# Sparse attention into a gated feed-forward layer: queries ordered by GpSimd, value maxima folded by VectorE, one lasting tile for value halves, first weight decoded in its own order

## The chip, the cores and the metric

One NeuronCore of a Trainium2 chip runs the whole program: TensorE (PE) multiplies, VectorE (DVE), ScalarE (ACT) and GpSimd (POOL) work elementwise, SyncE (SP) issues transfers. The metric is the device time of one execution in microseconds, the lower the better.

## The reference

Block-sparse attention over 4 batches, 8 heads, 768 positions and 64 channels, in 24 blocks of 32; then a feed-forward layer with a gate.

```python
scores = scale * np.matmul(q, k.transpose(0, 1, 3, 2))          # scale = 1/8
mask = (np.abs(blk_i - blk_j) <= 1) | (blk_i == 0) | (blk_j == 0) | (blk_i == 23) | (blk_j == 23)
for qb in range(24):                                            # and three drawn blocks a row
    for kb in sampled_blocks[qb]:
        mask[qb * 32:(qb + 1) * 32, kb * 32:(kb + 1) * 32] = True
attn = softmax(where(mask, scores, -1e9))
x = (attn @ v).transpose(0, 2, 1, 3).reshape(3072, 512)
h = x @ w_in                                                    # 512 x 2048
sp = np.maximum(h, 0.0) + np.log1p(np.exp(-np.abs(h)))
out = (h * erf(sp)) @ w_out                                     # 2048 x 512
```

The weights are float64, all else float32.

## The kernel before, in words

**Numbers.** Products of float32 accuracy are made from float16 halves: a value is scaled by a power of two and cut into a high half (a cast by ScalarE) and a low half (what is left, by VectorE), and three products of halves are added up in PSUM. Scores are float32 products.

**Weights.** Float64 weights arrive as pairs of 32-bit words, and `decode` (a `TENSOR_SCALAR` and two `SCALAR_TENSOR_TENSOR` on VectorE for each 1024 columns) puts float32 numbers together from them: 8 decodes for w_in (`key` is "i", i = 0, 2, ..., 14), 8 for w_out. Raw w_in lies partly in the places of w_out, so a w_out block is loaded (`load_w`, from ScalarE's queue) when the raw words there are decoded. `square` sums squares for the scales, `high` casts the high half (ScalarE), and the low half is made for w_in on TensorE: `rest` multiplies the float32 weight by a diagonal of scales, `rest_low` takes the high half off, `rest_out` casts. `weights()` is a generator; `later(n)` lets it go on by n steps.

**Attention.** A batch has 11 units of two query blocks each ("m") and 4 units for the first and last block ("f"); together 60 units. For a unit: `order_q` copies its queries from `qt`, the loaded tile, to `qm` (two tiles, used in turns; two copies of 64x256), `gather` copies the drawn key blocks `kg` (six copies on GpSimd for the unit's two blocks), `gather_v` loads value rows `vbuf` (SP, and an indirect transfer on GpSimd), `scores` writes `s_m` or `s_f` in PSUM, `soft_max` finds the row maximum `mx`, `soft_exp` the exponentials `pf` and their high half, `soft_low` the low half `p_m` and their transpose by DMA, `values` (three units later) writes `po`, `norm` divides (`rinv`, `xf`), `turn` cuts into halves and transposes.

**Values.** Values of the next batch are prepared while a batch runs (`behind`): `max_v` finds the largest magnitude of a batch's values, over the columns on VectorE and then over the 128 partitions, `scale_v` makes a power of two of it, `split_v` writes halves into a tile `vn`, with two columns of ones (a memset on GpSimd), and stores them to a table `vtab` in DRAM from which `gather_v` reads.

**Feed-forward.** x comes in 12 chunks of 256 rows; w_in's 2048 columns are taken in 8 groups of 256. `ff_first` writes h (24 products), `ff_logs`, `ff_power`, `ff_exp` and `ff_gate` compute the gate in turns on ScalarE and VectorE (tiles x, s, g), `ff_second` adds into o three groups later. That makes 96 groups in the main loop, and a table says in which iterations a unit of attention runs beside a group.

**Order.** Ahead of the loop six units and the weights run in an order that a scheduler sets for TensorE, ScalarE and VectorE; from the fourth iteration of the loop on these too follow the program. The queues of SP and GpSimd always do. A DMA queue waits at a transfer whose place is not free, and what stands behind it waits too. Every operation is recorded under one line, L47, so the rows below are told apart by tiles.

## Time and profile before

| | us |
|---|---|
| median of three executions (lowest, highest) | 804.48 (802.73, 805.50) |
| the profiled execution | 807.05 |
| its span in the trace | 804.5 |
| TensorE busy | 717.3 (89%) |
| VectorE busy | 646.8 (80%) |
| ScalarE busy | 601.0 (75%) |
| GpSimd busy | 209.2 (26%) |

The span reaches from the first to the last instruction that the trace holds, the execution's time has a little more around it. Busy shares are means over the whole span; the loop starts with the first h at 116 us, and the first o at 135 us.

### The profile page before, as it was taken

What the parts mean: (1) busy time and instruction counts of PE and PEld (TensorE: products, weight loads), DVE (VectorE), ACT (ScalarE), POOL (GpSimd) and SP (SyncE); (2) the same over time, 40 slices, a digit from 0 to 9 for tenths busy, and PEclk for the clock granted to TensorE, in tenths of its full rate; (3) what the DMA queues carried; (4) which work ended last, traced back from release to release, by engine and by line L of the source; (5) the groups of instructions that cost most, each with busy time, mean ns of one, the idle gap of its engine ahead of it and who ended that gap; (6) DMA issues with size and microseconds to landing.
All of it is one profiled execution on the core that took longest, in us unless ns stands there. A gap on an engine that the chain in (4) does not pass through costs nothing.

```text
span 804.5 us, 26510 instructions
## 1 busy us (share of the span) xinstructions
PE 717.3 (89%) x11136; PEld 505.3 (63%) x11136; DVE 646.8 (80%) x1215; ACT 601.0 (75%) x1035; POOL 209.2 (26%) x397
## 2 busy tenths in 40 slices
PE   1237888889977999999999899999999999999997
PEld 1235546656755777666767667667777776666663
DVE  5897999988878788887778888787888888775664
ACT  2556899678766788787857987887888788787674
POOL 2247721213334241500143424110344310000000
PEclk9658999989999999999999999999999999999999
DMA  9999853996699698953597998744598747312000
GB/s 307 405 196 321 245 110 74 210 214 156 135 234 213 146 243 183 198 122 81 131 195 169 201 240 182 167 110 102 126 188 179 155 115 172 74 33 43 8 27 26
DMA packets 187287, 129.46 MB, mean 161 GB/s; under 512 B 137760, under 2 KB 160928, under 8 KB 185376
## 3 DMA queue, kind: packets, MB, share of 16 engines
q1 hardware_dynamic: 173440, 83.98, 50.2%
q10 hardware_dynamic: 7840, 25.96, 10.2%
q0 software_dynamic: 5888, 17.84, 8.7%
q8 instruction: 87, 1.43, 0.7%
q14 instruction: 32, 0.26, 0.1%
HBM read 82.81 MB, written 12.95 MB: 119 GB/s over the span
## 4 chain that ended last, share of the span: by engine, by line
PE 68%; issue 11%; DVE 7%; DMA 4%; POOL 4%; ACT 3%; POOLq 1%; SPq 1%; ACTq 0%; DVEq 0%
PE h L47 27%; PE o L47 27%; PE s_m L47 7%; PE po_None L47 4%; PE s_f L47 3%; POOL vbuf L47 2%; POOL kg L47 2%; DMA qt<-in_qT_dram 2%; PE po L47 1%; DVE s L47 1%; DVE vn L47 1%; DVE p_m L47 1%; ACT x L47 1%; DMA vtab<-vn 1%; DMA pT_f<-p_f 1%
## 5 line engine op out<-in xcount | busy, mean ns | idle before, releaser
L47 PE MATMUL h<-xT,wi 128*128 128x256 f16 x2304 | 270.2, 274 | 7.1 <-DVE s L47 7.0
L47 PE MATMUL o<-wo,g 128*128 128x512 f16 x1152 | 268.4, 383 | 0.3 <-DVE g L47 0.2
L47 PEld LDWEIGHTS <-wi 128*128 128x128 f16 x2304 | 226.6, 99 | 56.3 <-issue 6.9
L47 PEld LDWEIGHTS <-g 128*128 128x128 f16 x1152 | 110.3, 99 | 123.8 <-issue 5.6
L47 POOL DMA_INDIRECT vbuf<-vtab,idx x88 | 94.7, 1076 | 322.4 <-PE po_None L47 254.5
L47 ACT ACTIVATE s<-s 128x512 f32<-128x512 f32 x192 | 120.1, 626 | 42.8 <-DVE s L47 33.5
L47 PE MATMUL s_m<-kx,qm 128*64 128x64 f32 (+1 forms) x1408 | 97.0, 250 | 35.9 <-DVE qm L47 17.2
L47 ACT ACTIVATE x<-x 128x512 f32<-128x512 f32 x192 | 121.1, 631 | 5.9
L47 POOL COPY kg<-kx 128x128 f32 x264 | 96.3, 412 | 69.9 <-PE s_m L47 54.5
L47 PEld LDWEIGHTS s_m<-kx,qm 128*64 128x64 f32 x1408 | 72.4, 148 | 42.6 <-issue 24.2
L47 ACT ACTIVATE pf_m<-s_m,nb_m 128x256 f32<-128x256 f32 x176 | 69.0, 475 | 38.7 <-DVE nb_m L47 38.5
L47 DVE SCALAR_TENSOR_TENSOR s<-x 128x512 f32<-128x512 f32 x96 | 67.5, 703 | 26.2 <-ACT x L47 26.1
L47 ACT ACTIVATE x<-h,isg 128x512 f32<-128x512 f32 x96 | 65.2, 679 | 30.7 <-PE h L47 30.6
L47 DVE SCALAR_TENSOR_TENSOR s<-s,s 128x512 f32<-128x512 f32 x96 | 67.7, 705 | 21.9 <-ACT s L47 18.5
L47 DVE SCALAR_TENSOR_TENSOR g<-s,sums,g 128x512 f16<-128x512 f32 x96 | 72.1, 751 | 3.4
L47 DVE TENSOR_REDUCE mx_m<-s_m 128x4 f32<-128x1024 f32 x44 | 53.7, 1221 | 23.2 <-PE s_m L47 22.9
L47 PE MATMUL s_m<-kg,qm 128*64 128x96 f32 x704 | 65.7, 261 | 6.7 <-issue 6.7
L47 DVE SCALAR_TENSOR_TENSOR s<-s,h 128x512 f32<-128x512 f32 x96 | 65.4, 681 | 0.5
L47 ACT ACTIVATE s<-x 128x512 f32<-128x512 f32 x96 | 60.4, 630 | 3.0
L47 DVE TENSOR_SCALAR g<-s,sums 128x512 f16<-128x512 f32 x96 | 47.4, 493 | 3.4
L47 DVE TENSOR_TENSOR p_m<-pf_m,p_m 128x1024 f16<-128x1024 f32 x38 | 49.5, 1303 | 0.4 <-ACT p_m L47 0.4
L47 PEld LDWEIGHTS s_m<-kg,qm 128*64 128x64 f32 x704 | 45.4, 149 | 5.5 <-issue 5.5
(109 smaller groups left out, 667.5 us busy)
## 6 DMA issues: line engine op xcount, KB each, us to landing
vbuf<-vtab SPq DMA_DIRECT2D x80, 195.0 KB, 4.5
vraw<-in_v_dram ACTq DMA_DIRECT2D x9, 768.0 KB
vtab<-vn SPq DMA_DIRECT2D x16, 390.0 KB, 3.3
vbuf<-vtab SPq DMA_DIRECT2D x12, 520.0 KB, 5.5
wo<-in_w_out_dram ACTq DMA_DIRECT2D x6, 1024.0 KB, 7.2
qt<-in_qT_dram SPq DMA_DIRECT2D x20, 256.0 KB
kr<-in_kT_dram ACTq DMA_DIRECT2D x12, 384.0 KB, 6.1
vbuf<-vtab SPq DMA_DIRECT2D x32, 130.0 KB, 6.2
```

The source lines that it names most:

```text
L47: done = call(*args, **kwargs)
```

## The change

Four parts. `order_q` runs on GpSimd for all units after the seventh of the first batch, and `next_queries` is cut in two: `order_next` (the copies) and `next_queries` (the loads), both called at the head of an iteration, ahead of its gathers, not at its end. For batches 1 to 3 the maximum over partitions is found by VectorE (`fold_bound`: transposes of 32x32 squares, reductions and copies) in place of a reduction by GpSimd. Where the halves of values went to a tile `vn` taken anew each time, there is one lasting tile, whose ones are set once. And w_in is decoded with its columns in the order in which they arrive, not with even and odd ones apart: `halves` reads the float32 numbers with a step instead, and `ff_first` counts columns accordingly.

```diff
--- before.py
+++ after.py
@@ -155,7 +155,9 @@
         qt = qts[b, t][:, :, half * 2 * BLOCK : (half + 1) * 2 * BLOCK].rearrange("p r (j c) -> p r j c", c=BLOCK)
         for a in range(2):
             place = qms[half][a * D : (a + 1) * D, :, :, a, :]
-            if b == 0 and 0 < u <= FIRST:
+            if b or u > FIRST:
+                pool.tensor_copy(place, qt[a * D : (a + 1) * D])
+            elif u:
                 act.activation(place, qt[a * D : (a + 1) * D], AF.Copy)
             else:
                 dve.tensor_copy(place, qt[a * D : (a + 1) * D])
@@ -181,23 +183,35 @@
 
     sums = cp.tile([P, 64], F32, tag="sums", name="sums")
 
-    def pow2_bound(bound, tag, by_sum):
+    def pow2_bound(bound, tag):
 
 
 
         top = st.tile([P, 1], F32, tag="top", name=f"top_{tag}")
         dve.reduce_max(top, bound, AX.X)
-        if by_sum:
-            allm = ps_h.tile([P, W], F32, tag="h", name=f"allm_{tag}")
-            if tag[0] == "v":
-                pe.matmul(allm[0:1, 1 : 1 + P], top, eye, start=True, stop=True)
-                top = st.tile([P, 1], F32, tag="top", name=f"most_{tag}")[0:1]
-                dve.reduce_max(top, allm[0:1, 1 : 1 + P], AX.X)
-            allm = allm[:, :1]
-            pe.matmul(allm, ones[: top.shape[0]], top, start=True, stop=True)
-        else:
-            allm = st.tile([P, 1], F32, tag="allm", name=f"allm_{tag}")
-            pool.partition_all_reduce(allm, top, P, bass.bass_isa.ReduceOp.max)
+        allm = ps_h.tile([P, W], F32, tag="h", name=f"allm_{tag}")
+        if tag[0] == "v":
+            pe.matmul(allm[0:1, 1 : 1 + P], top, eye, start=True, stop=True)
+            top = st.tile([P, 1], F32, tag="top", name=f"most_{tag}")[0:1]
+            dve.reduce_max(top, allm[0:1, 1 : 1 + P], AX.X)
+        allm = allm[:, :1]
+        pe.matmul(allm, ones[: top.shape[0]], top, start=True, stop=True)
+        return allm
+
+    def fold_bound(bound, tag):
+
+        one, other = fold[:, :BLOCK], fold[:, BLOCK:]
+        dve.reduce_max(one[:, :1], bound, AX.X)
+        dve.transpose(other, one)
+        most = st.tile([P, 5], F32, tag="most", name=f"most_{tag}", bufs=1)
+        for n in range(4):
+            dve.reduce_max(most[0:1, n : n + 1], other[n * BLOCK : n * BLOCK + 1], AX.X)
+        dve.reduce_max(most[0:1, 4:5], most[0:1, :4], AX.X)
+        dve.tensor_copy(other[0:1], most[0:1, 4:5].to_broadcast([1, BLOCK]))
+        dve.transpose(one[:BLOCK], other[:BLOCK])
+        allm = st.tile([P, 1], F32, tag="allm", name=f"allm_{tag}", bufs=1)
+        for n in range(4):
+            dve.tensor_copy(allm[n * BLOCK : (n + 1) * BLOCK], one[:BLOCK, :1])
         return allm
 
     def pow2_scale(allm, tag, squared):
@@ -224,6 +238,10 @@
         for quad in range(2):
             pool.dma_start(vtab[b][NB * BLOCK :, quad * QW : (quad + 1) * QW], zero16)
 
+    vn_of = cp.tile([P, KT, 2, VW], F16, tag="vn", name="vn_of")
+    pool.memset(vn_of[:, :, :, D : D + 2], 1.0)
+    fold = cp.tile([P, 2 * BLOCK], F32, tag="fold", name="fold")
+    dve.memset(fold, 0.0)
     vmax = {}
 
     def max_v(b, quad):
@@ -234,7 +252,7 @@
                 vmax[b][:, 4 * quad + h : 4 * quad + h + 1], vr, AX.X, apply_absolute_value=True
             )
         if quad == 1:
-            vscale[b] = pow2_bound(vmax[b], f"v{b}", b == 0)
+            vscale[b] = (fold_bound if b else pow2_bound)(vmax[b], f"v{b}")
 
     def scale_v(b):
         vscale[b] = pow2_scale(vscale[b], f"v{b}", False)
@@ -243,8 +261,11 @@
 
         s = vscale[b][0]
         place, bufs = ("vn", 1) if b else (("xT", 3), ("xT", 3), ("vn", 1), ("pf", 2))[2 * quad + half]
-        vn = (mo if place == "xT" else at).tile([P, KT, 2, VW], F16, tag=place, name=f"vn_{b}_{quad}_{half}", bufs=bufs)
-        pool.memset(vn[:, :, :, D : D + 2], 1.0)
+        if place == "vn":
+            vn = vn_of
+        else:
+            vn = (mo if place == "xT" else at).tile([P, KT, 2, VW], F16, tag=place, name=f"vn_{b}_{quad}_{half}", bufs=bufs)
+            pool.memset(vn[:, :, :, D : D + 2], 1.0)
         for a in range(2):
             vr = vraws[b, quad][half * 2 + a].rearrange("p (k d) -> p k d", d=D)
             hi, lo = vn[:, :, a, :D], vn[:, :, a, D + 2 :]
@@ -425,15 +446,7 @@
             dve.tensor_scalar(m, hi, 3, 0x3FFFFFFF, ALU.logical_shift_left, ALU.bitwise_and)
             dve.scalar_tensor_tensor(m, hi, -0x40000000, m, ALU.bitwise_and, ALU.bitwise_or)
             done = w32[:, c : c + w].bitcast(I32)
-            if key == "i":
-                lo, m = (x.rearrange("p (q e) -> p e q", e=2) for x in (lo, m))
-                done = done.rearrange("p (e q) -> p e q", e=2)
-            if key == "i" and i == 0:
-                part = mags[1][:, c : c + w]
-                dve.tensor_scalar(part.rearrange("p (e q) -> p e q", e=2), lo, 29, None, ALU.logical_shift_right)
-                dve.tensor_tensor(done, part.rearrange("p (e q) -> p e q", e=2), m, ALU.bitwise_or)
-            else:
-                dve.scalar_tensor_tensor(done, lo, 29, m, ALU.logical_shift_right, ALU.bitwise_or)
+            dve.scalar_tensor_tensor(done, lo, 29, m, ALU.logical_shift_right, ALU.bitwise_or)
             c += w
 
     def square(key, i):
@@ -444,7 +457,11 @@
 
     def halves(key, i):
         t, t16 = (wi, wi16) if key == "i" else (wo, wo16)
-        return t[:, i + APART[key], :], t16[:, i, :512], t16[:, i, 512:]
+        w32, hi16, lo16 = t[:, i + APART[key], :], t16[:, i, :512], t16[:, i, 512:]
+        if key == "i":
+            w32 = w32.rearrange("p (n q e) -> p n e q", n=2, e=2)
+            hi16, lo16 = (x.rearrange("p (n e q) -> p n e q", n=2, e=2) for x in (hi16, lo16))
+        return w32, hi16, lo16
 
     def scale_of(key, i):
         n = i // (2 * NK) if key == "i" else i // 2
@@ -481,7 +498,7 @@
         scale_part(total, n)
 
     def bound_part(part):
-        return pow2_bound(wsq["i"][:, part * NK : (part + 1) * NK], f"wi{part}", True)
+        return pow2_bound(wsq["i"][:, part * NK : (part + 1) * NK], f"wi{part}")
 
     def scale_half(total, part):
         scale_part(total, NP + part)
@@ -504,10 +521,10 @@
         pe.matmul(rests[i], diag, halves("i", i)[0], start=True, stop=False)
 
     def rest_low(i):
-        pe.matmul(rests[i], less16, halves("i", i)[1], start=False, stop=True)
+        pe.matmul(rests[i], less16, wi16[:, i, :512], start=False, stop=True)
 
     def rest_out(i):
-        act.activation(halves("i", i)[2], rests.pop(i), AF.Copy)
+        act.activation(wi16[:, i, 512:], rests.pop(i), AF.Copy)
 
     assert NK * NG == NF == 16
 
@@ -724,7 +741,7 @@
         for j in range(FG):
             hj = h[:, j * CW : (j + 1) * CW]
             for kt in range(NK):
-                i, c = (fg // 4) * 2 * NK + 2 * kt + j, (fg % 4) * P
+                i, c = (fg // 4) * 2 * NK + 2 * kt + fg % 4 // 2, (2 * (fg % 2) + j) * P
                 hi, lo = wi16[:, i, c : c + P], wi16[:, i, 512 + c : 512 + c + P]
                 p2_, a = divmod(kt, 2)
                 xa, xb = (xT[:, x * 2 + p2_, :, a * 64 : a * 64 + 64] for x in range(2))
@@ -821,13 +838,17 @@
             vfree -= 1
             most -= 1
 
-    def next_queries(m):
+    def order_next(m):
 
         b, n = divmod(m, per)
         if n < NU:
             order_q(b, n + 1)
         if n == NU + 1 and b + 1 < B:
             order_q(b + 1, 0)
+
+    def next_queries(m):
+
+        b, n = divmod(m, per)
         if n < NU - 1 and n % 2 == 0 and (b or n >= 6):
             load_q(b, n // 2 + 1)
         if n == NU - 1 and b + 1 < B:
@@ -934,6 +955,7 @@
             scores(unit)
             used_keys(unit)
             soft_max(unit)
+            order_next(begun)
             next_queries(begun)
             soft_exp(unit, True)
             soft_turn(unit)
@@ -975,6 +997,9 @@
         old = unit_of(begun - PV_LAG) if steps and begun - PV_LAG >= SEEN else None
         place = seen(old) if old else None
         begun += steps
+        if unit:
+            order_next(begun - 1)
+            next_queries(begun - 1)
         if group:
             ff_first(*group)
             ff_logs(*group)
@@ -1009,7 +1034,6 @@
             ff_exp(*group)
         open_unit = unit
         if unit:
-            next_queries(begun - 1)
             behind(begun - 1)
```

How rows move on three queues. Names end in numbers of tiles (batch, unit, running number).

ScalarE, ahead of the loop, where the first block of w_out is loaded. Before:

```order
L47 ACTIVATE qm0_97<-qt_0_2_135 64x8x32 x2
L47 DMA raw_14_304<-in_w_out_dram 128x1024
L47 ACTIVATE sq_i10_516,sums_101<-wi_108 128x1024
L47 DMA wo_109<-in_w_out_dram 128x2048
L47 ACTIVATE pf_m_0_2_660<-s_m_0_2_629,nb_m_0_2_656 128x256 x4
L47 ACTIVATE wi_108<-wi_108,sums_101 128x512
L47 ACTIVATE sq_i12_718,sums_101<-wi_108 128x1024
```

After:

```order
L47 DMA raw_14_306<-in_w_out_dram 128x1024
L47 ACTIVATE sq_i10_517,sums_101<-wi_112 128x1024
L47 ACTIVATE pf_m_0_2_661<-s_m_0_2_630,nb_m_0_2_657 128x256 x4
L47 ACTIVATE wi_112<-wi_112,sums_101 128x512
L47 DMA wo_113<-in_w_out_dram 128x2048
L47 ACTIVATE sq_i12_719,sums_101<-wi_112 128x1024
```

The load of `wo` stands behind the exponentials of unit 2 and the first cast.

VectorE in the loop, where the maximum of batch 1's values is found. Before:

```order
L47 SCALAR_TENSOR_TENSOR s2_0_0_4_2234<-s1_0_0_4_2073,s2_0_0_4_2234 128x512
L47 COPY qm0_97<-qt_0_5_2039 64x8x32 x2
L47 TENSOR_REDUCE vmax_1_1768<-vraw_1_1_2042 128x1 x4
L47 TENSOR_REDUCE top_v1_2251<-vmax_1_1768 128x1
L47 TENSOR_SCALAR m_v1_2255<-allm_v1_2253 128x1
```

After:

```order
L47 SCALAR_TENSOR_TENSOR s2_0_0_4_2237<-s1_0_0_4_2076,s2_0_0_4_2237 128x512
L47 TENSOR_REDUCE vmax_1_1769<-vraw_1_1_2043 128x1 x4
L47 TENSOR_REDUCE fold_110<-vmax_1_1769 128x1
L47 STREAM_TRANSPOSE fold_110<-fold_110 128x32
L47 TENSOR_REDUCE most_v1_2254<-fold_110 1x1 x4
L47 TENSOR_REDUCE most_v1_2254<-most_v1_2254 1x1
L47 COPY fold_110<-most_v1_2254 1x32
L47 STREAM_TRANSPOSE fold_110<-fold_110 32x32
L47 COPY allm_v1_2262<-fold_110 32x1 x4
L47 TENSOR_SCALAR m_v1_2267<-allm_v1_2262 128x1
```

The query copies are gone, and thirteen operations stand between the column maxima and `m_v1`.

GpSimd at about the same place in the program (units 7 to 10 of batch 0). Before:

```order
L47 DMA vbuf0_91<-vtab_0_102,idx_260 96x1040
L47 DMA vbuf1_92<-vtab_0_102,idx_260 96x1040
L47 ISA
L47 ISA allm_v1_2253<-top_v1_2251 128x1
L47 DMA vbuf2_93<-vtab_0_102,idx_260 96x1040
L47 DMA vbuf3_94<-vtab_0_102,idx_260 96x1040
L47 MEMSET vn_1_1_0_2471 128x12x2
L47 COPY kx_1_2478<-kr_1_0_2263 128x24x32
L47 MEMSET vn_1_1_1_2657 128x12x2
L47 COPY kx_1_2478<-kr_1_1_2480 128x24x32
```

After:

```order
L47 COPY qm0_97<-qt_0_5_1819 64x8x32 x2
L47 DMA vbuf0_91<-vtab_0_102,idx_264 96x1040
L47 DMA vbuf1_92<-vtab_0_102,idx_264 96x1040
L47 COPY qm1_98<-qt_0_5_1819 64x8x32 x2
L47 DMA vbuf2_93<-vtab_0_102,idx_264 96x1040
L47 DMA vbuf3_94<-vtab_0_102,idx_264 96x1040
L47 COPY kx_1_2488<-kr_1_0_2275 128x24x32
L47 COPY kx_1_2488<-kr_1_1_2490 128x24x32
L47 COPY qm0_97<-qt_1_0_2279 64x8x32 x2
```

A pair of query copies stands ahead of each iteration's gathers; the all-reduce and the memsets are gone.

## Rows read from the trace of the kernel before

**Rows 1.** The page, part 1: busy us of each engine over the whole span, with its share and the number of instructions.

```profile
PE 717.3 (89%) x11136; PEld 505.3 (63%) x11136; DVE 646.8 (80%) x1215; ACT 601.0 (75%) x1035; POOL 209.2 (26%) x397
```

**Rows 2.** Busy time by stretches of the span (us from its start): the stretch, its length, then busy us and instructions of each engine, the granted TensorE clock as a share of full speed, the DMA engines' mean share, GB/s.

```profile
0.00:64.00 64.00, 19.72 (x216) 17.32 (x217) 51.48 (x98) 27.62 (x53) 23.07 (x45) 0.73 0.96 306
64.00:80.00 16.00, 10.08 (x257) 7.01 (x256) 11.33 (x17) 10.49 (x22) 10.57 (x23) 0.89 1.03 314
80.00:136.00 56.00, 47.24 (x766) 32.46 (x765) 53.98 (x127) 52.12 (x101) 21.84 (x36) 0.97 0.59 147
136.00:182.00 46.00, 39.50 (x665) 26.89 (x664) 39.88 (x78) 33.54 (x59) 8.36 (x12) 0.93 0.93 197
182.00:804.50 622.50, 600.72 (x9238) 421.58 (x9235) 490.10 (x898) 477.21 (x804) 145.41 (x284) 0.99 0.66 141
```

**Rows 3.** What TensorE waited for after 136 us: tile to be written <- what ended the wait: us in total, times, longest us.

```profile
PE s_m L47 <- issue: 11.1, 4, 5.3
PE h L47 <- DVE s L47: 4.2, 3, 2.1
PE po L47 <- issue: 2.8, 1, 2.8
PE s_f L47 <- DVE qm L47: 2.5, 1, 2.5
```

**Rows 4.** Groups of VectorE instructions in the first 80 us, shapes kept apart: out <- in, shapes, count | busy us, mean ns | idle us before them. `room` is scratch, `wi` and `wo` the places of the weights (raw w_in lies in either).

```profile
L47 DVE SCALAR_TENSOR_TENSOR wi<-wo,room 128x1024 int32<-128x1024 int32 x4 | 8.1, 2014 | 0.0
L47 DVE SCALAR_TENSOR_TENSOR wi<-wi,room 128x1024 int32<-128x1024 int32 x3 | 6.0, 2012 | 0.0
L47 DVE TENSOR_SCALAR room<-wi 128x1024 int32<-128x1024 int32 x5 | 4.0, 809 | 0.0
L47 DVE SCALAR_TENSOR_TENSOR wo<-wo,room 128x1024 int32<-128x1024 int32 x2 | 2.5, 1230 | 0.0
L47 DVE TENSOR_TENSOR wi<-room 128x1024 int32<-128x1024 int32 x1 | 1.2, 1226 | 0.0
```

**Rows 5.** VectorE in order of time at two places ahead of the loop: start us, us, instruction [idle before <- what ended it].

```profile
63.88 0.70 DVE L47 TENSOR_SCALAR room<-wo 128x1024 int32<-128x1024 int32 x1 [0.27 <-DMA wo<-in_w_out_dram]
...
79.43 0.16 DVE L47 TENSOR_SCALAR rinv_None<-po_None 128x4 f32<-128x4 f32 x1 [1.77 <-PE po_None L47]
```

**Rows 6.** The query tile qm, VectorE's instructions: count, ns min/median/max, first and last start, forms; below, what VectorE waited for ahead of them.

```profile
L47 DVE COPY qm<-qt x84: 272/291/380, 15.4 to 666.9; 64x256 f32<-64x256 f32 x84
...
  DMA qt<-in_qT_dram: 4.6, 3
```

**Rows 7.** ScalarE in order of time: the issue of the first w_out block (ACTq is its DMA queue).

```profile
56.86 0.33 ACTq L47 DMA_DIRECT2D wo<-in_w_out_dram  x1
```

**Rows 8.** DMA issues from 54 to 80 us: out <- in, queue, count, KB each, median us from issue to landing.

```profile
wo<-in_w_out_dram ACTq DMA_DIRECT2D x4, 1024.0 KB, 7.0
```

**Rows 9.** Busy time by stretches, columns as in rows 2.

```profile
48.00:52.00 4.00, 2.38 (x32) 2.13 (x28) 4.00 (x6) 1.38 (x4) 0.93 (x1) 0.75 0.22 56
```

**Rows 10.** Groups of ScalarE instructions in the first 136 us: the casts of w_in to its high half.

```profile
L47 ACT ACTIVATE wi<-wi,sums 128x512 f16<-128x512 f32 x16 | 11.8, 738 | 0.6 <-PE rest L47 0.5
```

**Rows 11.** Groups of GpSimd copies, whole span, shapes kept apart.

```profile
L47 POOL COPY kg<-kx 128x128 f32 x264 | 96.3, 412 | 69.9 <-PE s_m L47 54.5 <-issue 10.6 <-DVE ix_room L47 2.7
L47 POOL COPY kx<-kr 128x768 f32<-128x768 f32 x12 | 10.8, 904 | 18.4 <-DMA kr<-in_kT_dram 18.4
```

**Rows 12.** VectorE in order of time from 141 to 175 us.

```profile
141.70 0.59 DVE L47 COPY qm<-qt 64x256 f32<-64x256 f32 x2
...
150.04 0.59 DVE L47 COPY qm<-qt 64x256 f32<-64x256 f32 x2 [0.78 <-DMA qt<-in_qT_dram]
...
152.63 0.16 DVE L47 TENSOR_REDUCE top_v<-vmax 128x1 f32<-128x8 f32 x1
153.34 0.15 DVE L47 TENSOR_SCALAR m_v<-allm_v 128x1 f32<-128x1 f32 x1 [0.55 <-POOL allm_v L47]
...
153.72 0.15 DVE L47 TENSOR_SCALAR s_v<-e_v 128x1 int32<-128x1 int32 x1
153.79 0.14 DVE L47 TENSOR_SCALAR i_v<-e_v 128x1 int32<-128x1 int32 x1
...
155.75 2.21 DVE L47 TENSOR_TENSOR p_m<-pf_m,p_m 128x1024 f16<-128x1024 f32 x1
...
163.85 1.15 DVE L47 SCALAR_TENSOR_TENSOR vn<-vraw,s_v,vn 128x384 f16<-128x384 f32 x2 [1.65 <-ACT vn L47]
...
174.70 0.68 DVE L47 SCALAR_TENSOR_TENSOR s<-s,h 128x512 f32<-128x512 f32 x1
```

**Rows 13.** TensorE in order of time, the two waits for s.

```profile
175.43 4.45 PE L47 MATMUL h<-xT,wi 128*128 128x256 f16 x24 [2.06 <-DVE s L47]
...
446.93 2.23 PE L47 MATMUL h<-xT,wi 128*128 128x256 f16 x19 [1.96 <-DVE s L47]
```

**Rows 14.** VectorE in order of time, the maximum for batch 3.

```profile
435.22 0.15 DVE L47 TENSOR_SCALAR m_v<-allm_v 128x1 f32<-128x1 f32 x1 [0.49 <-POOL allm_v L47]
```

**Rows 15.** GpSimd in order of time.

```profile
156.04 0.83 POOL L47 COPY kx<-kr 128x768 f32<-128x768 f32 x1
170.80 0.12 POOL L47 MEMSET vn<- 128x24 f16 x1 [13.93 <-DMA vtab<-vn]
```

**Rows 16.** The tile p_m, VectorE's instructions, columns as in rows 6.

```profile
L47 DVE TENSOR_TENSOR p_m<-pf_m,p_m x38: 1212/1218/2205, 109.0 to 669.3; 128x1024 f16<-128x1024 f32 x38
```

## The prediction

> **What bounds the kernel now.** I read the page's busy shares first: TensorE 717.3 us of the 804.5 us span, VectorE 646.8, ScalarE 601.0, GpSimd 209.2 [rows 1]. An average like that hides stages, so the busy time by stretches comes next [rows 2]. From 182 us on TensorE works 600.72 of 622.5 us, while VectorE works 490.10 and has 132 us to spare: there only what stops TensorE counts. Before that it is another kernel. In the first 64 us TensorE works 19.72 us, VectorE 51.48 and the DMA engines have a share of 0.96; from 64 to 80 us the DMA share is 1.03 and VectorE has 4.7 us idle; from 80 to 136 us VectorE works 53.98 of 56 us and ScalarE 52.12; from 136 to 182 us neither TensorE (39.50) nor VectorE (39.88 of 46) is full, so there a chain of waits sets the time.
>
> The waits of TensorE after 136 us come third [rows 3]. The largest, 11.1 us in four pieces and 2.8 us in one, stand under "issue": nothing that the profile shows ended them, and no part of the change touches a cause that I can name. Those that this change can touch are 2.5 us of s_f for queries (qm) by VectorE and 4.2 us of h for s by VectorE, together 6.7 us. So the loop can give back little, and the rest has to come from an earlier start of the loop.
>
> **First weight decoded in its own order.** The last step of a decode of w_in, today written with a 16-byte step between the elements it reads, takes 2014 ns (four times) or 2012 ns (three times); the same operation for w_out, in its own order, takes 1230 ns. The first decode (i = 0) does it with a TENSOR_TENSOR of 1226 ns and a TENSOR_SCALAR ahead of it; that the five TENSOR_SCALAR average 809 ns where the w_out ones take 700 ns [rows 4, 5] puts the extra one at 5 x 0.809 − 4 x 0.70 = 1.25 us. The saving on VectorE is 7 x 0.79 + 1.25 = 6.8 us, all of it before 63.9 us. Two pairs of query copies (unit 7, and unit 8 just ahead of the loop) also leave the part before the loop: 2 x 0.58 = 1.2 us, from a median of 291 ns for each of the two copies of a pair [rows 6].
>
> Does it reach the loop? After the last w_in decode VectorE already waits 0.27 us at 63.88 us for the first block of w_out, and at 79.43 us it waits 1.77 us for po, the product with the values of unit 1 [rows 5]. The block's load is issued by ScalarE at 56.86 us [rows 7] and such loads take 7.0 us to land in this stretch [rows 8]. If VectorE arrives 5.7 us earlier, at about 58, the wait grows unless the load goes out earlier too; and the row order of ScalarE shows it behind two more pieces of work, four exponentials and one cast. I put its issue at 55.4 us, 1.5 us earlier, so VectorE's gain of 5.7 us there shrinks to 1.5. What can move beyond that is bounded by transfers: the DMA engines are full to 80 us but for the stretch from 48 to 52 us, with a share of 0.22 [rows 9], that is 3.1 us of all engines' time. It ends when the gathers of values start, which need the halves of the values written by VectorE up to 40 us, and these come about 2.8 us earlier (the decodes i = 0 and i = 2 lie ahead of them: 1.25 + 2 x 0.79). Everything behind that gap, the values of unit 1 included, can so move by some 3 us. I take **−3.0 us** for the start of the loop. Bounds: 0, if the transfers end at 80 us as now; −8.0 (6.8 + 1.2), if nothing is late.
>
> The price of the new order is that the casts (high) and the f32 product rest read every second element, 8 bytes apart. No row of before shows ScalarE or TensorE with such a read. The decode's reads of the low words have that very step on VectorE and run at 1230 ns for 1024 elements, the full rate of a two-input operation here, and only the 16-byte step costs 2014. I take 0; the bound is the same factor, 2014/1230 = 1.64, on the 16 casts of 738 ns [rows 10]: +7.5 us on ScalarE.
>
> **Queries by GpSimd.** The 82 copies of 64x256 f32 leave VectorE and go to GpSimd. It copies 128x128 in 412 ns in the mean (contention included) and 128x768 in 904 [rows 11]; by size a 64x256 copy lies between, at about 0.45, 0.9 us for the pair; 41 pairs add 37 us to an engine that is busy 26%. They are issued at the head of the iteration, before that iteration's key and value gathers on GpSimd's queue, and the load of the next queries moves up on SP's queue ahead of the value loads and transposes. GpSimd's queue now waits for a query tile (VectorE does so three times today, 4.6 us [rows 6]), and the gathers queue behind. They are for units three iterations ahead, so a wait of 2 us is hidden; SP's load waits for copies that in turn wait only for the scores of the unit before. Cost 0, bound a few us in either direction, within the range.
>
> In the stretch where VectorE's chain sets the end (136 to 182 us) the pair at 141.70 (0.59), the one at 150.04 (0.59 with 0.78 of waiting for its transfer) and the one at 161.62 go away [rows 12]. The third brings nothing: right behind it VectorE waits 1.65 us for ScalarE (vn). So −2.0. That removes the 2.5 us of s_f at 162 us too, but TensorE then stands a little later at 175.43 us, where h waits for s from 174.70 [rows 12, 13]: the chain counts, not its waits one by one.
>
> **Maximum over partitions by VectorE.** For batches 1 to 3 one reduction, GpSimd's all-reduce and a wait, 0.71 us from top_v (152.63) to m_v (153.34), become thirteen small operations. Dependent small operations follow each other here every 0.19 us (153.34 to 153.72 are two steps) and independent ones every 0.07 us (153.72 to 153.79) [rows 12]. Seven dependent steps and six that follow freely make 7 x 0.19 + 6 x 0.07 = 1.75, some more for the 128x32 transpose: 1.9 us, so +1.2 in each of three places. (Bounds: 13 x 0.07 = 0.9, or 13 x 0.19 = 2.5, that is +0.2 to +1.8.) In the first place −2.0 + 1.2 = **−0.8**. In the second, for batch 3, up to 435.22 us [rows 14], one qm pair before it goes (−0.58): **+0.6**, and it does reach TensorE, which waits 1.96 us for s at 446.93 [rows 13]. The one for batch 2 lies in a stretch where TensorE doesn't wait for VectorE: 0.
>
> **One lasting place for the halves.** Thirteen of the sixteen memsets on GpSimd go; one of them held the queue 13.93 us up to 170.80 [rows 15] until the earlier halves were stored. ScalarE, which writes the halves next, must wait for the same store, so their time is unchanged. Behind the memset only a key copy for batch 1 was late, needed long after. 0.
>
> **Sum**: −3.0 − 0.8 + 0.6 = −3.2 us. The trace is of an execution of 807.05 us with a span of 804.5; the runs shown have a median of 804.48. The difference is taken off the median: **801.3 us**.
>
> **The rivals.**
> *The start gains in full*: the w_out blocks and values land as early as they are wanted. −8.0 − 0.2: 796.3 us. For it, VectorE is the busiest engine of the first 64 us (51.48 [rows 2]); against it, the waits for DMA at 63.88 and 79.43.
> *Nothing arrives*: transfers hold the start, and the loop gives −0.2: 804.3. For it, the DMA share of 1.03 up to 80 us.
> *The strided reads cost* (slower): the 16 casts take the factor 1.64 and ScalarE, busy 52.12 of 56 us from 80 to 136, passes it on: −3.2 + 7.5, 808.8 us. It decides from (806.9 − 801.3)/16 = 0.35 us per cast on. For it, the 2014 ns; against it, that 8-byte reads on VectorE are at full rate.
> *GpSimd's copies hold VectorE* (little change or slower): at 155.75 a two-input operation p_m took 2.21 us, its median is 1.22 [rows 12, 16], while GpSimd copied 0.83 us at 156.04 [rows 15]: as much as 1.0 us lost. If each pair of copies costs VectorE 0.9 us where it saves 0.58, five iterations before 182 us lose 5 x 0.9 = 4.5 us of the sum: −3.2 + 4.5, 805.8. Against it: a copy meets VectorE only when a two-input operation on SBUF runs, and reductions of scores (1.22 each) fill that time. The Trainium skill, page "SBUF — State Buffer", section "SBUF: two separate sides", calls the port that the two engines share an exclusive lock, held for a whole instruction by a GpSimd operation or a VectorE one with two inputs in SBUF, while the other stands still; the 2.21 us agrees, and by that rule alone this rival would be likelier than 0.12.
>
> **Chances.** Forecast 0.42 (own range 798.5 to 804), full gain 0.20, nothing 0.16, strided 0.10, held 0.12. The bound between change and no change is 0.3%, 2.4 us, about what this measurement can tell: below 802.1 faster, above 806.9 slower. Faster: two thirds of the first, the second and a little of the third, 0.51. Slower: the strided case, half of the last and 0.02 for an unlucky "issue" gap (their longest is 5.3 us [rows 3]), 0.18. Same: 0.31. The range reaches into both outer cases, 794.5 to 808.
>
> **What would show it.** Right: wi's last step at 1.22 us; VectorE waiting some 4 us for w_out near 58 us; the loop's first iterations about 3 us earlier; casts still 0.74; the fold in 1.9 us. Wrong: casts over 1.1 us; p_m and s<-x stretched beside qm copies in most units; gathers late with TensorE waiting for vbuf or kg; new or longer "issue" gaps.

## The result: slower, and the profile after

The changed kernel took 812.12 us (median of 17 executions, 805.74 to 829.09) where the kernel before took 805.11 (median of 17, 800.06 to 814.99): a ratio of 1.008, 95% interval 1.0052 to 1.0108. Forecast were 801.3 us. The profiled execution took 814.66 us, its span is 812.9.

Kernels were measured in groups (e1 to e4, e5 to e8, e9 to e12, e13 to e16, e17 and e18), each on one chip with the kernel before beside it. With the result and with e9 to e12 the kernel before took 805 to 806 us, with the other groups 817 to 818; a ratio is always to the kernel before of its own group. Ratios leave disturbed executions out; for e14 that takes so many away that its ratio, 1.0004, lies far below that of the medians of all executions, 1.0055. The loss is not the same in every group: the whole change gave 1.0038 (1.0001 to 1.0076) in e9 and 0.9982 (0.9951 to 1.0013) in e13.

The changed kernel's busy shares (the page's part 1, against [rows 1]) and its stretches ([rows 2]; columns as there):

```profile
PE 723.1 (89%) x11136; PEld 508.6 (63%) x11136; DVE 619.5 (76%) x1169; ACT 602.5 (74%) x1035; POOL 242.9 (30%) x464
...
0.00:64.00 64.00, 23.55 (x316) 17.84 (x316) 47.34 (x101) 29.61 (x56) 22.64 (x50) 0.84 0.97 315
64.00:80.00 16.00, 9.26 (x158) 6.16 (x159) 8.29 (x16) 8.81 (x18) 7.48 (x18) 0.68 1.00 286
80.00:136.00 56.00, 43.03 (x597) 29.18 (x597) 49.10 (x114) 49.29 (x94) 24.93 (x40) 0.88 0.51 143
136.00:182.00 46.00, 41.49 (x767) 29.75 (x767) 40.27 (x86) 34.71 (x61) 11.77 (x15) 0.96 0.93 187
```

VectorE lost 27 us of work, as intended, and GpSimd gained 34. But in each of the first three stretches VectorE stands idle longer: 16.7 us instead of 12.5, 7.7 instead of 4.7, 6.9 instead of 2.0. The same in one row each, from the start to the first o (busy us of PE, PEld, DVE, ACT, POOL). Before:

```profile
L47 PE MATMUL o<-wo,g x36: 379/379/390, 135.2 to 155.1; 128*128 128x512 f16 x36
0.00:135.20 135.20, 76.25 (x1233) 56.43 (x1234) 115.99 (x240) 89.69 (x173) 54.98 (x101) 0.85 0.82 242
```

After:

```profile
L47 PE MATMUL o<-wo,g x30: 379/379/390, 142.6 to 160.0; 128*128 128x512 f16 x30
0.00:142.60 142.60, 82.44 (x1232) 58.36 (x1232) 111.24 (x240) 93.47 (x178) 56.23 (x108) 0.83 0.76 231
```

4.8 us less work on VectorE, 12.2 us more idle time (31.4 instead of 19.2), and the first o comes 7.4 us later. Two more traces of the changed kernel have it at 144.0 (e9) and 140.6 us (e13), a second one of the kernel before at 136.9 (e5).

The loop's first h, though, comes 8.6 us earlier, not later. Before, then after:

```profile
L47 PE MATMUL h<-xT,wi x2304: 269/273/421, 116.1 to 789.2; 128*128 128x256 f16 x192
L47 PE MATMUL h<-xT,wi x2304: 269/273/422, 107.5 to 797.6; 128*128 128x256 f16 x192
```

In both kernels four groups of h (24 products each) stand ahead of the first o. TensorE in order of time at the fourth, and a stretch of 12 us around it (columns as in [rows 2]). Before:

```profile
129.61 2.79 PE L47 MATMUL h<-xT,wi 128*128 128x256 f16 x24 [2.82 <-DVE s L47]
124.00:136.00 12.00, 9.18 (x200) 7.87 (x199) 11.54 (x31) 11.71 (x22) 2.05 (x2) 1.00 0.37 75
```

After (`total` are the sums for the scales of the weights):

```profile
127.31 1.92 PE L47 MATMUL total<-sums,room 128*128 128x1 f32 x8 [3.71 <-ACT wi L47]
134.64 5.23 PE L47 MATMUL h<-xT,wi 128*128 128x256 f16 x24 [5.41 <-DVE s L47]
128.00:140.00 12.00, 6.59 (x58) 4.80 (x61) 11.81 (x33) 11.22 (x21) 0.00 (x0) 0.51 0.36 77
```

After, TensorE waits 3.7 us for ScalarE's work on w_in and 5.4 us for VectorE; from 124 to 136 us it works 3.3 of 12 us. The granted clock from 128 to 140 us is 0.51, the lower of its two levels (1.2 GHz), where before had 1.00 (2.4 GHz), and the same 24 products take 5.23 us instead of 2.79. So of the 7.4 us some 5.0 are the later start of the fourth group and 2.4 its slower products.

What becomes of the 7.4 us is read from ScalarE's issues of output stores, the first of the third and of the eighth chunk. Before, then after:

```profile
334.61 0.35 ACTq L47 DMA_DIRECT2D out_dram<-wi  x1
616.40 0.34 ACTq L47 DMA_DIRECT2D out_dram<-wi  x1
```

```profile
338.95 0.35 ACTq L47 DMA_DIRECT2D out_dram<-wi  x1
624.80 0.34 ACTq L47 DMA_DIRECT2D out_dram<-wi  x1
```

The distance is 4.3 us at the third chunk and 8.4 at the eighth, and from there to the end both take 188.1 us. So in this pair of traces some 3 us of the late start are caught up, and 4.1 us are lost anew between the third and the eighth chunk. Other traces do not repeat the split: the third chunk's store goes out at 340.39 us in e9, at 333.61 in e13, and at 339.19 in e5, the kernel before once more. TensorE's waits after 136 us (against [rows 3]):

```profile
PE h L47 <- DVE s L47: 9.8, 3, 3.6
PE s_m L47 <- issue: 4.4, 4, 1.7
PE h L47 <- DMA xT<-x: 3.8, 1, 3.8
PE po L47 <- DMA pT_f<-p_f: 3.2, 1, 3.2
PE po L47 <- issue: 2.9, 1, 2.9
```

The 11.1 us under "issue" shrink to 4.4 and the wait for qm is gone, but h waits 5.6 us longer for s, and two transfers (xT and pT_f) are waited for 7.0 us. All waits of that view, small ones included, add up to 25.2 us, before to 23.6: the waits change place more than they grow.

### The profile page after: what moved, and what is told of

Same layout as the page of the kernel before. It is cut to its first block, busy times and chain, and to the rows that moved or that the text cites. A ratio compares the mean times of both kernels' runs of the same rounds, so it can differ in the third digit from the quotient of the medians.

```text
span 812.9 us, 26495 instructions
## 1 busy us (share of the span) xinstructions
PE 723.1 (89%) x11136; PEld 508.6 (63%) x11136; DVE 619.5 (76%) x1169; ACT 602.5 (74%) x1035; POOL 242.9 (30%) x464
## 3 DMA queue, kind: packets, MB, share of 16 engines
q8 instruction: 87, 1.43, 0.7%
## 4 chain that ended last, share of the span: by engine, by line
PE 72%; DVE 11%; DMA 10%; ACT 3%; issue 3%; SPq 1%; POOL 0%; POOLq 0%; ACTq 0%; DVEq 0%
PE h L47 28%; PE o L47 25%; PE s_m L47 8%; PE po_None L47 4%; PE s_f L47 3%; DMA vbuf<-vtab 2%; DMA vbuf<-vtab,idx 2%; PE rest L47 2%; DVE s L47 2%; DMA qt<-in_qT_dram 1%; PE po L47 1%; DVE room L47 1%; DVE mx_m L47 1%; DMA pT_f<-p_f 1%; DMA wo<-in_w_out_dram 1%
## 5 line engine op out<-in xcount | busy, mean ns | idle before, releaser
L47 PE MATMUL h<-xT,wi 128*128 128x256 f16 x2304 | 274.6, 277 | 19.1 <-DVE s L47 15.2
L47 PE MATMUL o<-wo,g 128*128 128x512 f16 x1152 | 264.9, 380 | 0.3 <-DVE g L47 0.2
L47 ACT ACTIVATE s<-s 128x512 f32<-128x512 f32 x192 | 120.3, 627 | 39.6 <-DVE s L47 29.9
L47 POOL DMA_INDIRECT vbuf<-vtab,idx x88 | 92.5, 1051 | 190.8 <-PE po_None L47 106.3
L47 POOL COPY kg<-kx 128x128 f32 x264 | 92.6, 396 | 47.9 <-issue 30.9
L47 POOL COPY qm<-qt 64x256 f32<-64x256 f32 x82 | 43.1, 525 | 161.2 <-DMA vbuf<-vtab,idx 107.8
L47 PEld LDWEIGHTS s_m<-kx,qm 128*64 128x64 f32 x1408 | 71.0, 145 | 19.2 <-ACT qm L47 11.3
L47 DVE TENSOR_TENSOR p_m<-pf_m,p_m 128x1024 f16<-128x1024 f32 x38 | 47.1, 1241 | 6.6 <-ACT p_m L47 6.6
```

Of the source, the lines that this page charges most:

```text
L47: done = call(*args, **kwargs)
```

## Where VectorE's time went: the experiments

**ScalarE stands still at a load.** ScalarE in order of time, where it issues blocks of w_out (ACTq), after:

```profile
57.30 0.33 ACTq L47 DMA_DIRECT2D wo<-in_w_out_dram  x1
67.69 0.34 ACTq L47 DMA_DIRECT2D wo<-in_w_out_dram  x1
68.07 0.86 ACT L47 ACTIVATE qm<-qt 64x256 f32<-64x256 f32 x2 [8.96 <-DMA wo<-in_w_out_dram]
```

and before:

```profile
63.81 0.86 ACTq L47 DMA_DIRECT2D wo<-in_w_out_dram  x2
```

Before, the third and the fourth block go out together. After, the fourth waits, and ScalarE does nothing for 8.96 us. In the program's instructions transfers take eight semaphores in turn, and the wait that the fourth block's load carries is for the semaphore of the second block: that load now stands eight transfers ahead of the fourth block's and stood seven ahead before, so the two share a semaphore only after. The second block (issued at 55.01) has to land first. Behind ScalarE's hold wait its transposed halves, and VectorE for them 5.2 us at 74.8; TensorE waits 6.0 us for ScalarE at 69.6. Pieces of the change, alone or left out, show what brings the hold; three kernels take it away.

e1, the decode alone in the kernel before (`decode`, `halves`, `rest_low`, `rest_out` and the column count in `ff_first` as in the diff above):

```diff
-                i, c = (fg // 4) * 2 * NK + 2 * kt + j, (fg % 4) * P
+                i, c = (fg // 4) * 2 * NK + 2 * kt + fg % 4 // 2, (2 * (fg % 2) + j) * P
```

> The kernel before with one part of the change alone: w_in decoded in its own order. Theory A (the loss is made ahead of the loop by this part: ScalarE's queue stands 9 us at the load of the fourth w_out block, which shares a transfer semaphore with the second block's, and all behind it is late): ScalarE idle 8 to 10 us before 68 us on the w_out transfer, the first o of the loop near 142 us (135.2 before, 142.6 after), time +6 to +8 us, ratio 1.008. Theory B (the loss comes from GpSimd's query copies and the fold in the loop): first o at 130 to 135 us and time -3 to 0 us.

Measured: 1.0053 (1.0025 to 1.0081), first o at 142.1 us, and the hold:

```profile
66.52 0.84 ACT L47 ACTIVATE qm<-qt 64x256 f32<-64x256 f32 x2 [7.52 <-DMA wo<-in_w_out_dram]
```

So the decode brings the hold, and by itself makes the kernel slower, though not clearly by more than the control e15 below, in which no engine computes more. e2, the change without the decode (queries, fold and tile), in two measurements:

```diff
-            dve.scalar_tensor_tensor(done, lo, 29, m, ALU.logical_shift_right, ALU.bitwise_or)
+            if key == "i":
+                lo, m = (x.rearrange("p (q e) -> p e q", e=2) for x in (lo, m))
+                done = done.rearrange("p (e q) -> p e q", e=2)
...
```

> The changed kernel with the old decode: queries by GpSimd at the head of the iteration, fold by VectorE and the lasting tile alone. Theory A: no long wait of ScalarE for a w_out transfer, first o at 134 to 136 us, time -1.5 to +0.5 us against before. Theory B: first o at 135 us but the loop 6 to 8 us longer, ratio 1.008.

> Queries, fold and tile of the change, with the decode of before. If the hold at the w_out load is the main loss: no hold, first o at 137 to 140 us, ratio 1.000 to 1.002 as in its first run (1.0008). If GpSimd's queries delay the start by themselves, as in the run with them alone (141.9, 1.0052): first o at 141 us or later, ratio 1.004 or more.

Measured: 1.0008 (0.9978 to 1.0039) and, as e16, 1.0009 (0.998 to 1.0039). No hold, yet the first o of e16 comes at 140.8 us. Each expectation of e16 is half right: the start is nearly as late as GpSimd's queries would have it (141 us or later), and the time is that of the kernel before. A late first o is not a late end.

e3 issues the fourth block from SP's queue, e6 (and e14) puts 512 bytes between the loads, so that they take different semaphores, and e7 is e6 with the queries of before:

```diff
-            act.dma_start(raw.rearrange("p (n c) -> p n c", n=2), rows)
+            (sp if i == 6 else act).dma_start(raw.rearrange("p (n c) -> p n c", n=2), rows)
```

```diff
...
                 load_w(*piece)
+            if n == 6:
+                act.dma_start(spare, wsq["i"][:, 6:7])
```

> The changed kernel with the fourth w_out block's load moved from ScalarE's queue to SyncE's, so that ScalarE can't stand at it; the rest as in the changed kernel, the order ahead of the loop set anew. Theory A: ScalarE's wait of 9 us before 68 us gone, first o 4 to 8 us earlier than in the changed kernel (135 to 138 us), time near before (-2 to +2 us). Theory A2 (not the wait but the order of TensorE's work, in which the sums for the last w_out scales stand behind the last rests and three h, sets the start): ScalarE's wait gone, but first o still at 140 us or later and time +4 us or more. Theory B: time unchanged from the changed kernel.

> The changed kernel with one transfer of 512 bytes more on ScalarE's queue, between the loads of the second and the third w_out block, so that the fourth block's load takes its turn one place later and waits for a small load of values, not for the second block. Theory A (the wait of 9 us makes the loss): ScalarE's wait before 68 us gone, first o at 131 to 136 us, 7 to 10 us earlier than in the changed kernel, time -4 to 0 us against before. Theory A3 (the wait is a symptom, transfers are full and set the start anyway): first o at 140 us or later, time +4 us or more.

> As the kernel with the blocks apart, but with the queries copied by VectorE at the end of the iteration as before: decode, fold and lasting tile alone. Theory A: first o at 131 to 136 us, time -5 to 0 us. Theory Q (the queries by GpSimd cost by themselves, since the second copy of a pair waits until the gathers of values that GpSimd issued before it have landed, 108 us of waiting in all): 3 to 5 us faster than the kernel with the blocks apart. If the queries cost nothing: equal to it within 1.5 us.

> The whole change, beside the next run. Theory of the hold: ScalarE waits some 9 us for a w_out transfer, first o at 142 to 144 us, ratio 1.004 to 1.009.

> The whole change with the two w_out loads on transfer semaphores of their own (a transfer of 512 bytes more). Theory of the hold: no such wait, ratio at least 0.3% below that of the whole change beside it. Rival (order dealt anew, the hold is worth little in the time because TensorE has rests and sums to do meanwhile): first o 2 to 4 us earlier, the ratio within 0.3% of the other's.

Measured: e3 1.006 (1.0025 to 1.0094), without the hold, first o at 146.3 us, as its theory A2 had it and not A; e6 1.0061 (1.0034 to 1.0088); e7 1.0038 (1.0007 to 1.0069); beside the whole change at 0.9982 (e13, 0.9951 to 1.0013), e14 gave 1.0004 (0.9971 to 1.0037). In e6 the third and fourth block go out together again,

```profile
57.38 0.97 ACTq L47 DMA_DIRECT2D wo<-in_w_out_dram  x2
```

and the first o comes at 140.3 us, with the old queries (e7) at 136.8; in e13, with the hold (6.53 us), at 140.6. The semaphore is the cause of the hold: it goes when the two loads are set apart. But no time comes back: e14 is not faster than e13 beside it. The theory that the hold is the loss falls. Nor is the hold the whole of the late first o: without it e6 still has 140.3 us, and only with the old queries as well (e7) is it at 136.8. Whether e7 is the faster of the two, as its theory Q had it, the overlapping intervals do not tell. e6 and e14 are one kernel, and their ratios differ by 0.57%: differences of half a per cent between groups are not read here.

**Queries by GpSimd.** GpSimd's copies in the changed kernel: count, ns min/median/max, and what GpSimd had waited for ahead of them:

```profile
L47 POOL COPY qm<-qt x82: 387/402/1427, 100.2 to 667.5; 64x256 f32<-64x256 f32 x82
...
  DMA vbuf<-vtab,idx: 107.8, 29
  DMA qt<-in_qT_dram: 39.0, 5
```

A copy takes 0.40 us in the median, near the forecast 0.45. But 29 of them wait for indirect gathers that GpSimd itself had issued earlier, 107.8 us in all: in the program the second copy of many pairs carries a wait for the semaphores of such gathers. Five wait for their query tile, 39.0 us. Four kernels:

e4, queries alone (the first, the last and the `order_q` part of the diff above); e10, queries by GpSimd at the head of the iteration for batches 1 to 3 only; e11, only the call moved, the copies on VectorE as before; e12, e6 with the queries of e10.

```diff
-            if b == 0 and 0 < u <= FIRST:
+            if b:
+                pool.tensor_copy(place, qt[a * D : (a + 1) * D])
+            elif 0 < u <= FIRST:
...
+        if unit and begun > per:
+            next_queries(begun - 1)
...
+        if unit and begun <= per:
+            next_queries(begun - 1)
         if unit:
-            next_queries(begun - 1)
```

> The kernel before with only the queries moved: copies on GpSimd, copies and loads at the head of the iteration. Theory A: first o at 134 to 136 us, time -2 to 0 us. Theory B, and the rival that GpSimd's copies hold VectorE: time +2 to +6 us, with two-input operations of VectorE stretched by 0.4 us or more beside the copies in most units.

> The kernel before with GpSimd copying queries, and at the head of the iteration, for batches 1 to 3 alone; ahead of batch 1 everything is as before. Theory of the start: first o at 135 to 137 us, ratio 0.998 to 1.002. Rival (GpSimd's copies and its late gathers cost time in the loop, some 0.1 us for each of 45 units): ratio 1.004 or more, with TensorE waiting for s_m, s_f or vbuf longer than the kernel before. Second rival (the freed 0.58 us on VectorE per unit are gained where TensorE waits for s): ratio 0.997 or less.

> The kernel before with the call for the next queries (copies and load) at the head of the loop's iteration, the copies still by VectorE and ScalarE. If the place of the call deals the order ahead of the first o anew: first o at 139 us or later, ratio 1.003 to 1.006, as the run with GpSimd's queries alone. If it is GpSimd's wait for its own gathers that delays the start: first o at 135 to 137 us, ratio 0.998 to 1.002.

> The changed kernel with the two transfers on ScalarE's queue apart (the 512 bytes of the run blocks_apart) and GpSimd's queries for batches 1 to 3 alone. Theory of the start: first o at 136 to 138 us, ratio to the kernel before 1.000 to 1.004, as the run with old queries and blocks apart (1.0038). If the loop gains by GpSimd's queries: 0.997 or less, and this version would be faster than both. If the loop loses by them: 1.007 or more.

Measured: e4 1.0052 (1.0025 to 1.008), first o at 141.9 us; e10 1.0046 (1.0007 to 1.0085), first o at 138.9; e11 1.0086 (1.0052 to 1.0121), first o at 136.6; e12 1.0132 (1.0094 to 1.0171), at 138.0; the whole change beside the last three (e9) 1.0038 (1.0001 to 1.0076), at 144.0.

> The whole change once more, beside the three that follow, on their chip. If the loss lies ahead of the first o (theory of the start): first o near 142.6 us as before, against 135.2 and 136.9 in the two traces of the kernel before, and a ratio of 1.006 to 1.010. If the loss depends on the chip: a ratio under 1.004.

The loop gains nothing by GpSimd's queries (the second rival of e10 falls, and e12 went the way that speaks of a loss). The first rival of e10 has the ratio it named, not its sign: TensorE has no wait for vbuf there, and its wait for s_m is 6.1 us where before had 11.1. e9 has the late first o that the theory of the start named and a ratio below the one it named. The first o and the time part company again: of the four in this group the one with the latest first o, e9, is not slower than any other. And moving a call that does the same work costs 0.86% with the first o where it was; neither of e11's two theories allowed that.

**Fold and tile.** e8 has these two parts alone (`fold_bound`, `vn_of`); e5 is the kernel before once more, for its trace.

```diff
-            vscale[b] = pow2_bound(vmax[b], f"v{b}", b == 0)
+            vscale[b] = (fold_bound if b else pow2_bound)(vmax[b], f"v{b}")
```

> The kernel before with the fold by VectorE and the lasting tile alone. By the prediction: the fold costs 0.6 to 1.2 us and the tile nothing, time 0 to +1 us. If GpSimd's 13.9 us wait at the memset was on the way: -2 to -4 us, which would also explain why the queries alone lose 4 us and the three parts together lose nothing.

> The kernel before, unchanged, for its trace on the same chip as the runs beside it. Whatever the theory: first o of the loop where the trace of before has it, 135 us, if the start doesn't depend on the chip; later by as much as the chip is slower, if transfers set the start.

Measured: e8 1.0024 (1.0001 to 1.0046), first o 138.5; the forecast 0 to +1 us (at most 1.0012) lies inside, and the gain by the lost memset wait did not come. e5, one execution, took 821.72 us beside a median of 817.31 for the same kernel. One execution can lie some 8 us off its kernel's median (e4's profiled one took 813.98, its median is 821.93), so a trace tells order and waits, and the ratios tell the time.

**Does VectorE's work ahead of the loop set the time at all?** Two mirror images and a control, all from the kernel before. e17 does one step of the w_in decode twice (8 times 1.226 us more), e18 leaves it out for w_in (the weights lose their signs), e15 has only the 512 bytes of e6.

```diff
             dve.scalar_tensor_tensor(m, hi, -0x40000000, m, ALU.bitwise_and, ALU.bitwise_or)
+            if key == "i":
+                dve.scalar_tensor_tensor(m, hi, -0x40000000, m, ALU.bitwise_and, ALU.bitwise_or)
```

```diff
-            dve.scalar_tensor_tensor(m, hi, -0x40000000, m, ALU.bitwise_and, ALU.bitwise_or)
+            if key == "o":
+                dve.scalar_tensor_tensor(m, hi, -0x40000000, m, ALU.bitwise_and, ALU.bitwise_or)
```

> The kernel before with one step of each w_in decode (1.226 us, eight times, the one for the sign) done twice: +9.8 us on VectorE ahead of 72 us, nothing else. If the start is carried to the end: first o some 6 to 10 us later, ratio 1.007 to 1.012. If it is absorbed later: first o later, ratio under 1.005, and the distance shrinks by the third chunk's stores (335 to 340 us).

> The kernel before with that step left out for w_in (the weights lose their signs): 9.8 us less on VectorE in the same place, the mirror image of the run beside it. If VectorE's work sets the start: first o 4 to 8 us earlier, ratio 0.990 to 0.996. If transfers of w_out set it, or the order dealt anew costs what the work gives: first o at 135 us or later, ratio 0.998 or more.

> The kernel before with the transfer of 512 bytes and nothing else. If an order dealt anew costs by itself: ratio 1.003 to 1.006. If only the edits themselves cost: 0.998 to 1.002, first o at 135 to 137 us.

Measured: e17 1.0108 (1.0071 to 1.0145), e18 1.0046 (1.0012 to 1.008), e15 1.0044 (1.002 to 1.0068). From the start to the first o (columns as above), e17, and its third chunk's first store:

```profile
0.00:143.20 143.20, 81.12 (x1233) 60.34 (x1234) 123.63 (x244) 90.37 (x175) 64.48 (x102) 0.86 0.80 233
340.20 0.35 ACTq L47 DMA_DIRECT2D out_dram<-wi  x1
```

e18, and its third chunk's first store:

```profile
0.00:133.30 133.30, 82.18 (x1232) 59.87 (x1232) 103.38 (x224) 85.49 (x166) 55.48 (x102) 0.83 0.78 240
339.57 0.35 ACTq L47 DMA_DIRECT2D out_dram<-wi  x1
```

e15, and its third chunk's first store:

```profile
0.00:143.60 143.60, 82.29 (x1232) 60.28 (x1232) 115.48 (x240) 91.18 (x176) 53.87 (x101) 0.82 0.76 228
339.00 0.35 ACTq L47 DMA_DIRECT2D out_dram<-wi  x1
```

Against the 135.2 us of before (136.9 in e5): 9.8 us more work leave VectorE's idle time at 19.6 us (19.2), and the first o comes 8.0 us later (6.3). 9.8 us less raise the idle time to 29.9 us, and the first o comes only 1.9 us earlier (3.6). So most of the work taken away comes back as idle time, and the kernel is slower by 0.46%, while the added work goes with a first o that is later by nearly as much and with 1.08% (8.8 us). But the control, in which no engine computes more or less, puts the first o at 143.6 us too and costs 0.44%, so the added work is not shown to be what moved e17's first o. In the control, as in the changed kernel, the first h comes earlier (110.5 us) and the fourth group of h takes 5.30 us; e16, without the decode, has 111.6 and 5.30. So neither is proper to the change. In time e17 stands 0.62% above e18 beside it, for 19.6 us more work, and the two intervals overlap at their ends.

And whether the first o is at 133.3 (e18), 136.9 (e5, store at 339.19), 143.2 (e17) or 143.6 (e15), the third chunk's store goes out at 339.0 to 340.2 us; e13 and e16, with the first o at 140.6 and 140.8, have it at 333.61 and 333.27. The loop's first chunks do not carry the start on. So e17 has the ratio of its first theory and the shrinking distance of its second: its trace, of its shortest execution (819.79 us, the median is 824.94), does not show the loss passing through the start.

Between the first and the third chunk the transfers are the likelier bound: before, from 199.0 to 334.6 us, the DMA share is 0.93 (the last but one number), and TensorE stands idle 11 us there.

```profile
199.00:334.60 135.60, 124.34 (x2273) 90.40 (x2270) 111.12 (x208) 100.09 (x177) 53.58 (x104) 0.96 0.93 189
```

That is read from the trace and was not tested by an experiment of its own. The traces also show where the groups differ: from the first to the third and on to the eighth chunk's store the kernel before takes 135.6 and 281.8 us in its first trace and 141.7 and 292.0 in e5; from there to the end, with a DMA share of 0.34 and 0.37, it takes 188.1 and 188.6.

**What stays open.** The cause of the loss. Nearly every edit costs 0.1 to 1.3%, the 512 bytes alone 0.44%; e1 (0.53%) and e4 (0.52%) are not clear of that, so neither the decode nor the queries are shown to cost time by what they compute. And the whole change costs 0.8 and 0.4% where the kernel before takes 805 us, and nothing (0.9982) where it takes 817. It may be that the order and the semaphores of the kernel before fall well together and any other deal of them less well; the runs agree with that, but none shows it. In the traces no single wait makes up the 4.1 us between the third and the eighth chunk. Before, then after:

```profile
334.61:616.40 281.79, 275.60 (x4391) 195.24 (x4392) 231.94 (x428) 223.67 (x378) 72.75 (x145) 0.99 0.74 157
338.95:624.80 285.85, 278.27 (x4451) 197.56 (x4437) 222.89 (x402) 224.22 (x378) 92.44 (x182) 0.99 0.68 155
```

2.7 of the 4.1 us are TensorE's work, with 60 more products in this stretch, and 1.4 us are idle time.

## Why the prediction was wrong, by its own steps

*The decode's saving* was right on VectorE. Its last step in the changed kernel (groups as in [rows 4]), and the cast with a step (ScalarE, up to 142 us):

```profile
L47 DVE SCALAR_TENSOR_TENSOR wi<-wi,room 128x1024 int32<-128x1024 int32 x4 | 4.9, 1214 | 0.0
L47 DVE SCALAR_TENSOR_TENSOR wi<-wo,room 128x1024 int32<-128x1024 int32 x4 | 4.8, 1210 | 0.0
```

```profile
L47 ACT ACTIVATE wi<-wi,sums 128x512 f16<-128x512 f32 x16 | 12.4, 775 | 2.5 <-PE rest L47 2.5
```

1.21 us where 1.22 was said; and VectorE waits for the first w_out block as forecast (some 4 us near 58):

```profile
61.29 0.75 DVE L47 TENSOR_SCALAR room<-wo 128x1024 int32<-128x1024 int32 x1 [4.03 <-DMA wo<-in_w_out_dram]
```

*−3.0 us for the start of the loop* is the step that failed: it took a gain at the start to pass on, to the first o and to the end. The first h did come earlier, by 8.6 us where 3.0 were said (bounds 0 to −8.0), but the first o came 7.4 us later. The argument that "everything behind that gap" moves with the halves of the values followed VectorE's and the transfers' times and left out the way from the first h to the first o: who issues the loads (one on ScalarE's queue that must wait stops ScalarE itself, here for 9.0 us), how the scheduler deals the casts and sums anew, and the lower clock that TensorE is granted around its waits there (2.4 us). These are what the trace shows for the first o; what made the kernel slower stays open, since without the hold it is no faster (e6, e14) and a late first o is not a late end (e16). The second half of the fault e18 shows alone: its first o comes earlier, and its end does not. The rival "nothing arrives" had this half of it, at 804.3 us, as the best that could come; it had no term for a loss.

Two readings inside the step were off as well. Ahead of the last half of the values (39.73 us) VectorE has done the first decode and one last step of 2.00 us (at 32.32), so the halves gain 1.25 + 0.79 = 2.0 us, not 2.8; they are done 2.2 us earlier (38.1 instead of 40.4). And the first block of w_out, said to be issued at 55.4 us, went out at 52.34 and reached VectorE at 61.29, 2.6 us earlier than before.

*Strided reads, 0 (bound +7.5)*: 775 ns where the cast took 738 [rows 10], 16 x 0.037 = 0.6 us. Right; the rival of 808.8 us did not happen, and that its time lies nearest to the result is chance.

*Queries, 0 elsewhere and −2.0 from 136 to 182 us*: the size of a copy was right; the waits of GpSimd for its own gathers, and of 39.0 us in five places for query tiles, were not seen, where a wait of 2 us had been reckoned with. "The third brings nothing" was right: VectorE, in order of time, now waits 0.50 us longer for vn than in [rows 12], where the pair gave 0.58.

```profile
156.04 0.16 DVE L47 TENSOR_REDUCE fold<-vmax 128x1 f32<-128x8 f32 x1
...
158.53 0.15 DVE L47 TENSOR_SCALAR m_v<-allm_v 128x1 f32<-128x1 f32 x1
...
168.12 1.15 DVE L47 SCALAR_TENSOR_TENSOR vn_of<-vraw,s_v,vn_of 128x384 f16<-128x384 f32 x2 [2.15 <-ACT vn_of L47]
```

*The fold, 1.9 us*: 2.49 from its first operation to m_v, so +1.8 in a place where +1.2 was said. Three of the four small reductions and three of the four copies had been counted at 0.07 us each, as if they followed freely; in this trace the four take 0.74 and 0.62 us. The bound, 2.5, just holds it.

*GpSimd's copies hold VectorE* did not show. p_m from 182 to 800 us, after and then before:

```profile
L47 DVE TENSOR_TENSOR p_m<-pf_m,p_m 128x1024 f16<-128x1024 f32 x33 | 40.9, 1240 | 6.6 <-ACT p_m L47 6.6
```

```profile
L47 DVE TENSOR_TENSOR p_m<-pf_m,p_m 128x1024 f16<-128x1024 f32 x33 | 42.4, 1286 | 0.0
```

Beside 82 more copies on GpSimd p_m takes no longer than before. The Trainium skill, page "SBUF — State Buffer", section "SBUF: two separate sides", would have it stretched, or the copy, by the exclusive lock; none of that shows in this mean. It may show on GpSimd's side, where a copy that began while p_m ran took 1.43 us and not 0.40:

```profile
148.34 1.22 DVE L47 TENSOR_TENSOR p_m<-pf_m,p_m 128x1024 f16<-128x1024 f32 x1
148.40 1.43 POOL L47 COPY qm<-qt 64x256 f32<-64x256 f32 x1 [4.54 <-DMA vbuf<-vtab,idx]
```

Which of the two gives way is not told by the starts: in [rows 12, 15] p_m began first as well, and was itself the longer one.

*The chances*: 0.18 for slower was too little, and the range's upper end, 808, lay under the result. It priced losses as longer operations; what the traces show ahead of the first o are engines standing still and TensorE at its lower clock.

## What to carry to other kernels

Before counting on work taken off a busy engine, see what it will wait for next, and test it with a mirror pair, the same work once added and once left out: here leaving it out gained nothing. Say which event a forecast start means and follow it to the end: here the first h came earlier, the first o later, and the time followed neither. Follow each load that an edit moves to the engine that issues it and to the transfer whose semaphore it has to wait for, since what stands behind it on that engine waits too. And in a kernel whose order is dealt by a scheduler, run an edit that adds no computing, as the 512 bytes here, to know what a few tenths of a per cent mean.

## What was not expected of the hardware and the program

A load that ScalarE issues held the engine for 6.5 to 9.1 us in four traces, until an earlier load with the same semaphore had landed, and a transfer of 512 bytes between them took that away. GpSimd's second copy of a pair waited for GpSimd's earlier gathers to land, 107.8 us in 29 waits; TensorE's waits after 136 us show none for the gathers. TensorE's granted clock was 0.51 from 128 to 140 us, where TensorE worked 3.3 of the 12 us from 124 to 136, and 24 products took 5.23 us instead of 2.79. And the kernel before took 805 us in some groups and 817 in others, where the changed one took 812 and 815.
